# Two layers of sliding-window attention and gated MLP on one core: nine ring units, the edge visit third, and smaller edge and V buffers

## The chip, the cores and the metric

The kernel runs on one core of a Trainium2 chip. The metric is the device time of one execution in microseconds, as the median over several executions.

## The reference

A tensor x of 2048 positions by 512 features passes twice through the same two blocks, with the same weights both times: `x = x + A(layernorm(x))`, then `x = x + B(layernorm(x))`.

- A is attention with 32 heads of 16 features over a causal window of 256 positions: `qkv = x @ wqkv`; scores `q k^T / 4`, masked to `0 <= query - key < 256`; softmax; times v; then `@ wo`.
- B is a gated MLP of width 1792: `h = sigmoid(x @ w_gate) * (x @ w_up)`, then `h @ w_down`.

Everything is stored in bf16.

## The kernel before

**Tiles.** Positions are cut into 16 tiles of 128 for each layer; j counts the 32 tiles of both layers. Q, K and the normalized rows are made for groups of four tiles (512 positions). For a tile of 128 keys, only the queries of this tile and the next two can see it. These are six half tiles of 64 queries: four of them lie inside the band and are stored in the score ring, and the two at its ends (the first half of the key tile itself and the last half of the tile two later) each matter for half of the keys. Those two ends are done together, as the edge.

**Visits.** The scores of a key tile are made in five visits, in an order that `visit_list` writes out. An A visit (number `cq`, 0 to 3) takes a quarter of the heads and four half tiles of queries: it fills all four score banks (`Sps`) with products on 32-row strips of TensorE (L1066). An R visit makes the edge for all heads (L1077). After each visit, ACT takes the exponential of all 2048 columns in one instruction (L1119) and writes it to `PTring` or to `edge`. The last tile of a layer has an R and an S visit (L1087). VectorE then multiplies by the masks (L997).

**Ring units.** `PTring` holds, for each head, `UNITS` slots of 64 queries. `UNIT[j]` names the four slots of tile j, in the order of the half tiles. A visit writes its slots in ascending order. Where the ascending order is not the order of the queries, or where the ring of queries `qT` wraps, `scores` cuts the visit into contiguous runs (`cut`); each run costs 8 products and 8 weight loads. `unit_table` searches for a table that keeps the slots free of collisions.

**Values.** When all exponentials and masks of a tile's window are there, `values` multiplies by V with a column of ones (L1146), for half of the heads at a time. `pv_done[tile, half]` tells of its end. From it, ring slots (`ring_free`), edge slots (`edge_slot`) and V buffers (`VP` pairs of tiles) become free. The result is turned by a DMA (or by TensorE for the first two tiles), divided by the sum, turned again and multiplied by wo (L929).

**MLP.** Gate and up products are L834, tanh is on ACT (L852), the multiplication on VectorE (L860), the down product L898. The groups of tiles for it are listed in `GLU`, and `OPT["g0"]` and `OPT["g2"]` choose one list for each layer.

**Order.** A planner (`Plan`) runs when the program is built. It keeps a model of the five engines and of the DMA queues; whenever a modelled engine is free, it issues the ready task of the best priority (`PRIO`, later `LATE_PRIO`). `pick` decides what TensorE does next: a visit when its pace (`PACE`) and the exponential before it allow, values when they are ready, otherwise a product of an open unit of Q, K (L736, L769), V (L806), wo, gate, up or down, by rank. Where nothing is ready at the start it issues products on the identity (L1329). So each engine has a fixed instruction stream, and in the program every instruction waits for its own semaphores.

**Start.** `loads` issues the first four tiles of x (`OPT["x0"]` chooses in which pieces), then the weights of K and of Q, each half on SP and half on ACT (L491). The layer norm of a tile is statistics on VectorE (L625, L626), an epsilon and a power on POOL (L634, L635), the application on VectorE (L653), and then a turn by TensorE (L674) or by DMA (L692). `by_tile` units of Q and K go through the group's four tiles one by one and can begin before all four are there; `OPT["bq"]` and `OPT["bk"]` say how many.

Of the kernel before, what the change touches and what calls it, by code (L numbers as in the profile page):

```python
# [13 lines left out]
P = 128  # L14
# [12 lines left out]
UNITS = 8  # L27
# [3 lines left out]
VP = 6  # L31
# [4 lines left out]
def unit_table():  # L36

    def taken(table, j):
        busy = set()
        late = j > 0 and (j - 1) % NT >= NT - 2
        for i in range(max(0, j - 3), j):
            for k, u in enumerate(table[i]):
                if i + (k + 1) // 2 >= j - late:
                    busy.add(u)
        return busy

    def choices(free, t):
        for x in sorted(free):
            if t == NT - 1:
                yield (x,)
            for a in range(1, UNITS):
                if t == NT - 2 and {x + a, x + 2 * a} <= free:
                    yield (x, x + a, x + 2 * a)
                for b in range(a + 1, UNITS):
                    quad = (x, x + a, x + b, x + a + b)
                    if t < NT - 2 and set(quad) <= free and (a == 1 or b == 2 * a or 2 * b == UNITS):  # L60
                        for q in permutations(quad):
                            if q[1] < q[2]:
                                yield q

    def extend(table):
        if len(table) == 2 * NT:
            return table
        for c in choices(set(range(UNITS)) - taken(table, len(table)), len(table) % NT):
            full = extend(table + [c])
            if full:  # L70
                return full
        return None

    return extend([])


UNIT = unit_table()


# [14 lines left out]
def pool_ns(n):  # L94
# [5 lines left out]
GLU = [[[1] * 4 + [4], [1] * 4 + [2] * 2, [1] * 6 + [2], [1] * 8], [[4] * 3 + [2, 1, 1], [4] * 3 + [2, 2], [4] * 4]]  # L100
PACE = [2621, 3006, 2055, 2786, 22]
# [9 lines left out]
RATE = ((10000, 280.0), (1e9, 345.0))  # L111
FIRST = 1500
# [6 lines left out]
PRIO = dict(st_x0=9.66, ap_x0=5.2, xt_x0=4.11, st_x1=6.83, ap_x1=4.97, xt_x1=-3.99, st_x=7.22, ap_x=1.33,  # L119
    xt_x=-1.25, st_p=4.93, ap_p=3.21, xt_p=5.11, st_g=6.44, ap_g=2.28, xt_g=4.67, st_g0=1.93, ap_g0=2.34,  # L120
    xt_g0=2.83, tp=5.29, tp_g=-2.14, q=6.35, q0=1.85, q1=2.88, k=3.53, k0=0.63, k1=0.73, s=-1.61, s0=0.46,
    s1=5.56, v=-1.31, v0=3.84, v1=8.0, vv=4.71, exp=4.44, exp0=6.15, m0=4.27, m00=-2.03, e0=3.94, e00=6.05,
    e1=4.23, e10=4.3, m2=0.81, m20=21.82, th=2.08, mu=-0.98, dn=2.02, add=5.32, add0=5.49, out=5.31, mv=6.36,
    mv0=3.86, oq=6.63, oq0=3.3, no=0.56, no0=0.37, on=-0.26, on0=4.14, vc=4.31, vc0=-2.12)
OPT = dict(gu='SP', g1=1, bk=1, bq=1, wide=0, r0=2, g0=1, g2=2, x0=2, eps=0, hold=0, own=0)
SLACK = dict(xt=1080, oq=240, on=28, vc=2480)
RANK = dict(tp=-2.963, o=1.872, lead=10.494, far=6.876, v=1.959, g=2.363, d=3.317, feed=14.564, x3=44361,
    wd=12, go=211)
LATE_PRIO = dict(st_p=4.07, ap_p=2.35, xt_p=6.18, st_x=1.67, ap_x=5.19, xt_x=-0.8, st_g=2.98, ap_g=1.19,
    xt_g=5.62, q=3.84, k=3, s=3, v=0.28, exp=3, m0=4.62, e0=1.63, e1=6, m2=6.84, th=3.38, mu=3.54, dn=2.85,  # L130
    add=0.69, out=5.87, mv=5.22, oq=0.1, no=4, on=1.28, vc=3.04)
LATE_SLACK = dict(xt=0, oq=1051, on=203, vc=0)
LATE_RANK = dict(tp=-2, o=1.5, lead=10, far=5.293, v=1.796, g=1.974, d=2.466, feed=22.042, go=1418)
# [271 lines left out]
class Net:  # L405


    def __init__(self, ctx, tc, A_x, wqkv, wo, w_gate, w_up, w_down, out):
# [28 lines left out]
        self.edge = big.tile([P, 6, H // 2, HP], BF16, name="edge")  # L437
# [290 lines left out]
    def q_unit(self, L, g, cq):  # L728
        nc, pl, key = self.nc, self.pl, ("p", L, g)
        t0, gi = g * NBG, L * NTG + g  # L730

        by_tile = L == g == 0 and cq < OPT["bq"]
        w = P if by_tile else TGW

        def steps(bank):
            return [(mm_ns(w), lambda kt=kt, o=o: nc.tensor.matmul(  # L736
                self.banks[bank][:, o:o + w], lhsT=self.wq[:, kt, cq * P:cq * P + P], rhs=self.xnT[key][0][:, o // P:(o + w) // P, kt, :],
                start=kt == 0, stop=kt == KT - 1)) for o in range(0, TGW, w) for kt in range(KT)]

        def evac(u):  # L740
            u.done.then(lambda: self.used(key, 1))
            d = pl.task({"ACT": act_ns(TGW), "DVE": dve_ns(TGW)}, lambda e: self.copy(
                e, self.qT[:, cq, gi % QG * TGW:(gi % QG + 1) * TGW].rearrange("p (t z k) -> p t z k", z=2, k=HP),
                self.banks[u.bank][:].rearrange("p (t k z) -> p t z k", z=2, k=HP)), [u.done], self.prio["q" + self.phase(L, g)])
            d.done.then(self.q_ready[L, g, cq].fire)
            return d.done

        tiles = [self.xn_ready[key, t] for t in range(t0, t0 + NBG)]
        needs = [self.has_wq["q"]] + ([] if by_tile else tiles)
        if gi >= QG:  # L750
            needs.append(self.seen[divmod((gi - QG) * NBG + NBG - 1, NT)])
        u = Unit(("q", L, g, cq), steps, needs, False, evac)
        if by_tile:
            u.want = [e for e in tiles for kt in range(KT)]
        return u

    def k_slots(self, j, n):
        a = min(n, KS - j % KS)
        return [(0, a, j % KS)] + ([(a, n - a, 0)] if n > a else [])

    def k_unit(self, L, g, cq):
        nc, pl, key = self.nc, self.pl, ("p", L, g)
        t0, gi = g * NBG, L * NTG + g

        by_tile = L == g == 0 and cq < OPT["bk"]
        w = P if by_tile else TGW

        def steps(bank):
            return [(mm_ns(w), lambda kt=kt, o=o: nc.tensor.matmul(  # L769
                self.banks[bank][:, o:o + w], lhsT=self.wq[:, kt, D + cq * P:D + cq * P + P], rhs=self.xnT[key][0][:, o // P:(o + w) // P, kt, :],  # L770
                start=kt == 0, stop=kt == KT - 1)) for o in range(0, TGW, w) for kt in range(KT)]

        def evac(u):
            u.done.then(lambda: self.used(key, 1))
            slots = self.k_slots(gi * NBG, NBG)

            def cp(e):
                for a, n, at in slots:
                    self.copy(e, self.kTp[:, cq, at:at + n, 0, :], self.banks[u.bank][:].rearrange("p (t k) -> p t k", k=P)[:, a:a + n, :])

            def split(e):
                for a, n, at in slots:
                    kt = self.kTp[:, cq, at:at + n]
                    for i in (1, 0):
                        nc.vector.tensor_scalar(out=kt[:, :, i, :], in0=kt[:, :, 0, :], scalar1=self.rms[i][:, 0:1], scalar2=None, op0=ALU.mult)  # L785

            a = pl.task({"ACT": act_ns(TGW), "DVE": dve_ns(TGW)}, cp, [u.done], self.prio["k" + self.phase(L, g)])
            b = pl.task({"DVE": 300 + 320 * len(slots)}, split, [a.done], self.prio["s" + self.phase(L, g)], port=True)
            b.done.then(self.k_ready[L, g, cq].fire)
            return a.done  # L790

        tiles = [self.xn_ready[key, t] for t in range(t0, t0 + NBG)]
# [3 lines left out]
        u = Unit(("k", L, g, cq), steps, needs, False, evac)  # L796
# [147 lines left out]
    def visit_list(self):  # L944
# [4 lines left out]
        for L in range(2):  # L949
            for t in range(NT):  # L950
                if t == NT - 1:
                    self.visits += [(L, t, "R", 0), (L, t, "S", 0)]
                    continue
                for cq in range(NCQ):
                    if cq == (OPT["r0"] if t == 0 else 0):
                        self.visits.append((L, t, "R", 0))
                    self.visits.append((L, t, "A", cq))

    def visit_needs(self, L, t, kind, i):
        needs = []  # L960
        for cq in ((i,) if kind == "A" else range(NCQ)):
            needs.append(self.k_ready[L, t // NBG, cq])
            for g in {t // NBG, min(NT - 1, t + 2) // NBG}:
                needs.append(self.q_ready[L, g, cq])
# [7 lines left out]
    def visit_exp(self, s):  # L972
# [9 lines left out]
        elif j >= 2:  # L982
            deps += [self.pv_done[divmod(j - 2, NT) + (h,)] for h in range(2)]
# [35 lines left out]
    def edge_slot(self, j, z):  # L1019
        return 2 + j % 4 if z else j % 2  # L1020
# [182 lines left out]
    def by_pe(self, L, t):  # L1203

        return L * NT + t < 2 or L * NT + t >= 2 * NT - 0
# [244 lines left out]
    def go(self, *srcs):  # L1450
# [12 lines left out]
        self.q_ready = {k + (c,): Event() for k in LG for c in range(NCQ)}  # L1463
        self.k_ready = {k + (c,): Event() for k in LG for c in range(NCQ)}
# [5 lines left out]
        for L, g in LG:  # L1470
            self.left["p", L, g] = 2 * NCQ + NBG
# [18 lines left out]
        for L, g in LG:  # L1490
            for cq in range(NCQ):
                ks.append(self.k_unit(L, g, cq))
                qs.append(self.q_unit(L, g, cq))
# [66 lines left out]
```

## Time and profile before

| | us |
|---|---|
| median of 6 runs | 543.67 |
| lowest and highest | 542.39, 545.09 |
| the profiled execution | 542.42 |
| its span, first to last instruction | 540.7 |
| TensorE busy in it | 532.3 |
| VectorE busy | 410.6 |
| ScalarE (ACT) busy | 384.2 |

The span is what the profile shows; the profiled execution's own time lies 1.7 us above it. PE stands for products on TensorE, PEld for its weight loads, DVE for VectorE, ACT for ScalarE, POOL for GpSimd, SP for SyncE, which issues most DMAs. A q behind an engine's name is its sequencer. "L1066" is a line of the kernel before. In a group's row the figures are: instructions, busy time in us, mean length of one in ns, and the idle time of the engine ahead of them. In the timeline the first two figures are the start and the length of a run of like instructions, whose first shape is the one printed. In the waits the three figures are the total in us, the number of times, and the longest.

### The profile page before, as it was taken

The page shows a single profiled execution, that of the slowest core. Times are in us where ns is not written, and L with a number is a line of the kernel's source. Part 1 is how long each engine was busy: PE and PEld are TensorE (multiplying, and loading weights), DVE is VectorE, ACT ScalarE, POOL GpSimd, SP SyncE. Part 2 cuts the span into 40 slices and gives each one's busy share as a digit, 9 for nine tenths or more (in the row PEclk, how much of TensorE's full clock was granted, in tenths as well). Part 3 has the DMA queues.
Part 4 walks back from the last instruction along what each step waited for, and adds up shares of the span by engine and source line. Part 5 has one row for each costly group of instructions (what it writes and reads, how often), then busy time and mean ns, then how long its engine had stood idle before and what let it go on. Part 6 is the DMA issues. An engine that isn't in the chain of part 4 may idle for free.

```text
span 540.7 us, 22638 instructions
## 1 busy us (share of the span) xinstructions
PE 532.3 (98%) x10298; PEld 288.3 (53%) x10298; DVE 410.6 (76%) x816; ACT 384.2 (71%) x374; POOL 45.0 (8%) x105
## 2 busy tenths in 40 slices
PE   7999999999999999999999999999999999999997
PEld 7446765867667554444444455544444444444443
DVE  6999989888888797698978788797777785552332
ACT  3998879889889787797679885788868774321320
POOL 6210201000001010001000001010000000000000
PEclk9999999999999999999999999999999999999999
DMA  8862232243311433172224420242223313211001
GB/s 271 306 139 100 42 71 42 65 81 54 71 44 33 82 41 62 26 118 51 42 32 71 80 53 20 38 98 51 52 52 80 42 41 70 51 19 35 6 11 39
DMA packets 95040, 36.31 MB, mean 67 GB/s; under 512 B 78304, under 2 KB 93920, under 8 KB 94944
## 3 DMA queue, kind: packets, MB, share of 16 engines
q1 hardware_dynamic: 93584, 33.56, 29.5%
q8 instruction: 80, 1.31, 1.0%
q10 hardware_dynamic: 1360, 1.31, 0.7%
q14 instruction: 16, 0.13, 0.1%
HBM read 9.70 MB, written 2.10 MB: 22 GB/s over the span
## 4 chain that ended last, share of the span: by engine, by line
PE 92%; DMA 3%; DVE 2%; ACT 2%; issue 1%; SPq 0%; POOL 0%; DVEq 0%; ACTq 0%
PE bank L834 36%; PE bank L898 18%; PE bank L1146 9%; PE Sps L1066 7%; PE bank L929 5%; PE bank L769 5%; PE bank L736 5%; PE bank L806 4%; PE Sps L1077 2%; DMA wq<-in_A_wqkv_dram 1%; ACT PTring L1119 1%; DMA xnT<-xn 1%; DMA OnT<-On 1%; SPq L491 0%; DVE kTp L785 0%
## 5 line engine op out<-in xcount | busy, mean ns | idle before, releaser
L1119 ACT ACTIVATE PTring<-Sps 128x2048 bf16<-128x2048 f32 (+1 forms) x122 | 226.2, 1854 | 61.7 <-PE Sps L1066 57.1
L834 PE MATMUL bank<-xnT,wg 128*128 128x512 bf16 (+2 forms) x672 | 126.0, 309 | 0.2 <-DMA xnT<-xn 0.2
L834 PE MATMUL bank<-xnT,wu 128*128 128x512 bf16 (+2 forms) x672 | 124.3, 308 | 0.0
L860 DVE SCALAR_TENSOR_TENSOR hT<-hT,bank 128x512 bf16<-128x512 bf16 (+1 forms) x140 | 78.8, 576 | 42.4 <-PE bank L834 36.0
L898 PE MATMUL bank<-wd,hT 128*128 128x512 bf16 (+2 forms) x462 | 109.8, 373 | 0.0
L852 ACT ACTIVATE hT<-bank 128x512 bf16<-128x512 f32 (+1 forms) x140 | 68.8, 517 | 52.2 <-PE bank L834 50.7
L834 PEld LDWEIGHTS <-wg 128*128 128x128 bf16 x672 | 55.3, 98 | 40.9 <-issue 1.5
L834 PEld LDWEIGHTS <-wu 128*128 128x128 bf16 x672 | 55.9, 98 | 39.4 <-issue 1.0
L898 PEld LDWEIGHTS <-hT 128*128 128x128 bf16 x462 | 42.7, 98 | 46.7 <-issue 0.4
L1119 ACT ACTIVATE edge<-Sps 128x2048 bf16<-128x2048 f32 (+1 forms) x32 | 56.7, 1773 | 12.9 <-PE Sps L1077 12.6
L997 DVE TENSOR_TENSOR PTring<-PTring,mask 128x1024 bf16<-128x1024 bf16 x64 | 43.9, 687 | 25.0 <-ACT PTring L1119 24.8
L1146 PE MATMUL bank<-PTring,Vaug 128*32 128x64 bf16 (+1 forms) x2880 | 52.8, 203 | 0.4 <-issue 0.4
L1066 PEld LDWEIGHTS <-kTp 32*128 32x128 bf16 x1984 | 25.6, 93 | 45.3 <-issue 43.3
L1146 PEld LDWEIGHTS <-Vaug 128*32 128x32 bf16 x2880 | 44.3, 97 | 9.6 <-issue 5.9
L1066 PE MATMUL Sps<-qT,kTp 32*128 32x64 bf16 (+3 forms) x1984 | 48.1, 215 | 0.9 <-issue 0.6
L634 POOL TENSOR_SCALAR st<-st 128x2 f32<-128x2 f32 (+1 forms) x37 | 13.1, 353 | 427.6 <-DVE st L626 427.6
L625 DVE BATCH_NORM_STATS2 st<-xsb 128x6 f32<-128x512 bf16 x64 | 43.9, 686 | 2.6 <-DMA xsb<-in_A_x_dram 2.2
L1146 PE MATMUL bank<-edge,Vl 128*32 128x64 bf16 x1024 | 44.4, 193 | 0.1
L704 DVE CAST OTs<-bank 128x512 bf16<-128x512 f32 x48 | 34.9, 728 | 8.6 <-PE bank L1146 8.6
L1146 PE MATMUL bank<-edge,Vh 128*32 128x64 bf16 x896 | 40.8, 193 | 0.3 <-issue 0.3
L997 DVE TENSOR_TENSOR edge<-edge,maske 128x1024 bf16<-128x1024 bf16 x60 | 40.4, 680 | 0.8 <-ACT edge L1119 0.7
L997 DVE TENSOR_TENSOR PTring<-PTring,maskn 128x1024 bf16<-128x1024 bf16 x56 | 38.1, 683 | 0.0
(71 smaller groups left out, 528.6 us busy)
## 6 DMA issues: line engine op xcount, KB each, us to landing
Vl<-Vaug SPq DMA_DIRECT2D x32, 68.0 KB, 2.4
out_dram<-xsb SPq DMA_DIRECT2D x15, 128.0 KB, 2.1
Vh<-Vaug SPq DMA_DIRECT2D x28, 68.0 KB, 2.5
wg<-in_B_w_gate_dram SPq DMA_DIRECT2D x2, 896.0 KB, 9.1
wu<-in_B_w_up_dram SPq DMA_DIRECT2D x2, 896.0 KB, 11.8
wd<-in_B_w_down_dram SPq DMA_DIRECT2D x7, 256.0 KB, 4.9
xsb<-in_A_x_dram SPq DMA_DIRECT2D x6, 256.0 KB, 7.3
wq<-in_A_wqkv_dram ACTq DMA_DIRECT2D x2, 256.0 KB, 5.7
```

The lines of the kernel that those rows point to most:

```text
L625: nc.vector.bn_stats(out=st[:, 0:6], in_=self.xsb[:, t, :])
L704: self.nc.vector.tensor_copy(out=out, in_=in_)
L736: return [(mm_ns(w), lambda kt=kt, o=o: nc.tensor.matmul(self.banks[bank][:, o:o + w], lhsT=self.wq[:, kt, cq * P:cq * P + P], rhs=self.xn ...
L769: return [(mm_ns(w), lambda kt=kt, o=o: nc.tensor.matmul(self.banks[bank][:, o:o + w], lhsT=self.wq[:, kt, D + cq * P:D + cq * P + P], rhs ...
L834: return [(mm_ns(w), lambda i=i, j=j, fc=fc, wt=wt, kt=kt: self.nc.tensor.matmul(pt[:, i, j, :], lhsT=wt[:, kt, fc * P:(fc + 1) * P], rhs= ...
L852: self.nc.scalar.activation(out=self.hT[:, ch[0] * GW:ch[0] * GW + size], in_=pt, func=AF.Tanh, scale=0.5)
L860: self.nc.vector.scalar_tensor_tensor(out=h, in0=h, scalar=1.0, in1=pt, op0=ALU.add, op1=ALU.mult)
L898: nc.tensor.matmul(self.banks[bank][:, 0:w], lhsT=self.hT[:, at:at + P], rhs=self.wd[:, fc, d], start=fc == 0, stop=fc == FC - 1)
L997: done = pl.task({"DVE": dve_bf_ns(1024)}, lambda e: nc.vector.tensor_tensor(out=r, in0=r, in1=m.to_broadcast([P, 16, HP]), op=ALU.mult), ...
L1066: nc.tensor.matmul(self.sps[:, m, o:o + n * HP], lhsT=kTp[32 * m:32 * m + 32, i, tt, e, :], rhs=self.qT[32 * m:32 * m + 32, i, q0:q0 + n * ...
L1119: nc.scalar.activation(out=out, in_=src, func=AF.Exp, scale=scale)
L1146: nc.tensor.matmul(o, lhsT=Va[:, c0:c0 + 32], rhs=p(h), start=k == 0 or t == 0, stop=k == len(parts) - 1 or t == 0, tile_position=(0, 32 * g))
```

## The change

- `UNITS` goes from 8 to 9, and the searched table is replaced by a table written out. With nine slots nearly all tiles get their four in the order of the queries.
- The R visit stands third in every tile (before the A visit with `cq` 2); before, it stood so in the first tile of each layer alone and was first in the others.
- The edge buffer has 5 slots instead of 6 (two for one end, three for the other instead of four). The exponential of an R visit waits for the values of the tile before (before: of the tile two before).
- V has five pair buffers instead of six.
- Q and K are told ready tile by tile and no longer by group: a visit needs K of its own tile and Q of its own and the next two tiles. The first two Q units of the first group can be cut into three tiles and one.
- Options at the start: three pieces of x instead of two (`x0=1`), three K units and two Q units of the first group by tile (`bk=3, bq=2`; before, one and one), the epsilon of the first group added on VectorE (`eps=1`), the first transposes in banks of their own (`own=1`).
- The last MLP group of layer two is two groups of two tiles (`g2=1`; before, one of four).
- The planner's paces, priorities, ranks and its model of the DMA rate at the start have other values. `turn=2` is what was there before.

```diff
-UNITS = 8
+UNITS = 9
-VP = 6
+VP = 5
...
-UNIT = unit_table()
+UNIT = [
+    (4, 5, 7, 8), (1, 2, 3, 4), (0, 1, 5, 6), (2, 3, 7, 8), (0, 1, 4, 5), (7, 2, 3, 6), (0, 1, 7, 8), (2, 3, 4, 5),
+    (1, 2, 6, 7), (1, 3, 4, 0), (1, 2, 5, 6), (3, 4, 7, 8), (0, 1, 2, 3), (4, 5, 6, 7), (0, 1, 2), (8,),
+    (3, 4, 5, 6), (0, 1, 7, 8), (2, 3, 4, 5), (1, 2, 6, 7), (1, 3, 4, 0), (1, 2, 5, 6), (3, 4, 7, 8), (1, 2, 3, 0),
+    (4, 5, 6, 7), (1, 2, 3, 4), (0, 1, 5, 6), (2, 3, 7, 8), (0, 1, 4, 5), (2, 3, 6, 7), (0, 1, 2), (8,),
+]
...
-PACE = [2621, 3006, 2055, 2786, 22]
+PACE = [2682, 3207, 1600, 2511, 23.52]
...
-RATE = ((10000, 280.0), (1e9, 345.0))
-FIRST = 1500
+RATE = ((3300, 330.0), (5300, 160.0), (1e9, 345.0))
+FIRST = 1100
...
-OPT = dict(gu='SP', g1=1, bk=1, bq=1, wide=0, r0=2, g0=1, g2=2, x0=2, eps=0, hold=0, own=0)
+OPT = dict(gu='SP', g1=1, bk=3, bq=2, wide=0, r0=2, g0=1, g2=1, x0=1, eps=1, hold=0, own=1, ck=0, cq=2,
+    turn=2)
...
-        self.edge = big.tile([P, 6, H // 2, HP], BF16, name="edge")
+        self.edge = big.tile([P, 5, H // 2, HP], BF16, name="edge")
...
+    def cut(self, L, g, cq, n):
+        return ((0, NBG - 1), (NBG - 1, 1)) if L == g == 0 and cq < n else ((0, NBG),)
...
-            d.done.then(self.q_ready[L, g, cq].fire)
+            d.done.then(lambda: [self.q_ready[L, t, cq].fire() for t in range(t0, t0 + n)])
...
-                    if cq == (OPT["r0"] if t == 0 else 0):
+                    if cq == OPT["r0"]:
                         self.visits.append((L, t, "R", 0))
...
-            needs.append(self.k_ready[L, t // NBG, cq])
-            for g in {t // NBG, min(NT - 1, t + 2) // NBG}:
-                needs.append(self.q_ready[L, g, cq])
+            needs.append(self.k_ready[L, t, cq])
+            needs += [self.q_ready[L, u, cq] for u in range(t, min(NT, t + 3))]
...
-        elif j >= 2:
-            deps += [self.pv_done[divmod(j - 2, NT) + (h,)] for h in range(2)]
+        elif j >= 1:
+            deps += [self.pv_done[divmod(j - 1, NT) + (h,)] for h in range(2)]
...
-        return 2 + j % 4 if z else j % 2
+        return 2 + j % 3 if z else j % 2
```

## The prediction

> **What bounds the kernel now.** I read the engine shares first, then the chain that ended last, then the products by shape, then TensorE's timeline, and last the first 13 us. From the page, parts 1, 2 and 4:
>
> ```profile
> PE 532.3 (98%) x10298; PEld 288.3 (53%) x10298; DVE 410.6 (76%) x816; ACT 384.2 (71%) x374; POOL 45.0 (8%) x105
> PEclk9999999999999999999999999999999999999999
> PE 92%; DMA 3%; DVE 2%; ACT 2%; issue 1%; SPq 0%; POOL 0%; DVEq 0%; ACTq 0%
> ```
>
> TensorE is busy from start to end, unthrottled, and is 92% of the chain. Busy time hides small stops in overlapping instructions, so I took the distances from one product's start to the next from the timeline. They are rigid: 216 ns between products 512 wide, 109 at 256, 56 at 128. TensorE is one belt: the span is the sum of what lies on it, the start before it runs, and 3.4 us after the last product (537.3 to 540.7). The stops on it are few. The waits of TensorE, all that were listed above 0.2 us:
>
> ```profile
> PE bank L1329 <- POOL ident L544: 1.4, 1, 1.4
> PE bank L1146 <- issue: 0.6, 2, 0.4
> PE Sps L1066 <- issue: 0.6, 1, 0.6
> PE bank L769 <- DMA wq<-in_A_wqkv_dram: 0.5, 1, 0.5
> PE bank L736 <- DMA wq<-in_A_wqkv_dram: 0.4, 1, 0.4
> ```
>
> Summing every distance that exceeds its normal one gives 3.0 us after 12.35 us. That, the start, and the products' own cost are all that an edit can move.
>
> **What the Trainium skill says.** "TensorE: Matmul & The Clock Gate", section "Wait — 56ns, not 53.3ns?", gives N/2.4 + 2.5 ns from start to start when warm, twice the array time when cold. The trace agrees: 216, 109 and 56; the filler products on the identity stand 107 apart until about 5.3 us. The same page, Part 3, section "The mechanism", has four 32-row tiles start about 4 ns apart and run together; here I read 3 to 4 ns within a group of four. "TensorEngine Tiling (Array Packing)", section "Key Properties", says that a change of tiling mode drains TensorE. The trace agrees: from a 512-wide product to the first score product are 312 ns instead of 216, so 96 ns. These three make a score visit cheap to cut and dear to enter.
>
> **The cuts of the visits.** Of a visit's queries each contiguous run costs 8 products and 8 weight loads. From the tables of ring units in both versions, with the wrap of the query ring of 24, I counted runs: before, 28 visits of tile 0 to 14 have one run of four (8 products), 52 have two (16), 20 have three (24), 12 have four (32), and 8 have one run of three. That is 1984 products, as the page's L1066 count has. After: 84, 24, 4, 0 and 8, which is 1216. So 768 products and 768 loads go. What is one worth? By form:
>
> ```profile
> L1066 PE MATMUL Sps<-qT,kTp 32*128 32x64 bf16 x1120 | 29.1, 190 | 0.6 <-issue 0.6
> L1066 PE MATMUL Sps<-qT,kTp 32*128 32x192 bf16 x480 | 21.8, 243 | 0.0
> L1066 PE MATMUL Sps<-qT,kTp 32*128 32x256 bf16 x224 | 11.1, 273 | 0.0
> ```
>
> The mean lengths tempt: 32 at 190 against 8 at 273. They overlap, so they are no price. The timeline has it, in start times (us) of a visit and of what follows it:
>
> ```profile
> 129.21 0.40 PE L1066 MATMUL Sps<-qT,kTp 32*128 32x256 bf16 x8
> 129.54 0.61 PE L834 MATMUL bank<-xnT,wu 128*128 128x256 bf16 x4
> ...
> 155.63 0.41 PE L1066 MATMUL Sps<-qT,kTp 32*128 32x64 bf16 x32
> 155.98 0.39 PE L834 MATMUL bank<-xnT,wu 128*128 128x256 bf16 x2
> ...
> 179.32 0.37 PE L1066 MATMUL Sps<-qT,kTp 32*128 32x64 bf16 x25
> 180.27 0.23 PE L1066 MATMUL Sps<-qT,kTp 32*128 32x64 bf16 x7 [0.58 <-issue]
> ```
>
> Eight products hold the belt 0.33 us, thirty-two 0.35. Medians over all visits: 329, 334, 340 and 344 ns for one to four runs, 275 for the run of three. Visits before: 28 x 329 + 52 x 334 + 20 x 340 + 12 x 344 = 37.5 us; after: 84 x 329 + 24 x 334 + 4 x 340 = 37.0 us. **-0.5 us**. The exponential of a visit (1.88 us for ring and edge alike) and its writes are unchanged. The third pair shows what else dense products can cost: two visits of four runs met a stop of 0.58 us that waits for nothing but issue. With 64 instructions fewer in a row there, I take it as gone: **-0.6 us**, bounds 0 and -1.5 (all four issue stops of that kind, the two larger in the rows above and 0.3 to 0.6 in between).
>
> **The other products.** Two K units and one Q unit of the first group go by tile: 16 x 56 = 896 ns instead of 4 x 216 = 864, three times: **+0.1 us**. The cut of Q's first group falls on units that go by tile anyway: nothing on the belt, two more copies on ACT or DVE (0.59 or 0.69 at full width), beside the products. The last MLP group of the second layer becomes two of two tiles: 224 products of 256 for 112 of 512, 224 x 109.5 against 112 x 216.5: **+0.3 us**. It can start sooner, but from 461 us on TensorE has no gap to fill, so the sooner start is worth nothing. The end stays 3.4 us: the last down product's split is not touched.
>
> **The start.** This is the largest term. The chain in order of time:
>
> ```profile
> 2.47 0.65 SPq L491
> 3.12 0.05 issue
> 3.17 7.51 DMA wq<-in_A_wqkv_dram
> 10.68 0.04 issue
> 10.72 0.51 PE bank L736 x6
> 11.23 0.22 PE bank L1329 x4
> 11.45 0.24 PE bank L674 x4
> 11.69 0.02 issue
> 11.71 0.59 ACT xnT L702
> 12.31 0.04 issue
> 12.35 0.38 PE bank L769 x4
> ```
>
> K's weights are there at 9.21 us, Q's at 10.72. Only one K and one Q unit could run by tile, tile 3's transposes stood in TensorE's queue behind Q products waiting for the weights (its normalized rows were ready at 9.84, its transposes began at 11.29), and the belt runs without filler only from 12.35. By then it had done 16 transposes, 12 K and 12 Q products, 40 x 56 = 2.2 us. After: three K units by tile have 48 products, 2.7 us, between the K and the Q weights. The added pair of x loads (one issue more on SP and one on ACT, 0.8 us each) is ahead of both weights on both queues; as the DMA engines are the limit from 5 us on (331 to 382 GB/s), I charge half, 0.4 us: K's weights at 9.6, Q's at 11.1. The epsilon on VectorE takes POOL's step out (0.32 us from its start to the next step's), and tile 0's normalization no longer stands behind tile 2's statistics (root done 5.82, applied 6.83); transposes are out of the way before 9.6. From 9.6 to 12.35 the belt then does 2.75 us on top of 0.9 us of transposes: 3.65 - 2.24 = **-1.4 us**. Bounds: -1.8 with no later weights; +0.8 if the pair delays them in full and the order of the queue wastes the rest.
>
> **Entries.** A block of value products that follows a visit pays no 96 ns of its own; 55 of 63 do so now. The new order can win or lose the other 8: -0.8 to +0.8 us, taken as nothing.
>
> **The moved edge visit.** Its 32 products (346 ns), exponential and two masks (0.68 us each on DVE) are the same, in third place. Its exponential now waits for both halves of the values of the tile before, where it waited for the tile two before; behind it on ACT stand copies and tanh, and the next visit's products, which need the score banks. In the trace of before the third visit's exponential starts 2.5 us (median) after the second half of the values of the tile before has ended; in two of 28 tiles (3 and 5) it starts 0.7 us sooner than that. So it binds twice: cost between 0 and 1.4 us, and MLP products are there to fill: nothing. V in five pairs: a V unit now waits for values seven tiles back instead of nine; in the trace only tiles 10, 12 and 13 of layer 0 were written before that point, by 9 to 13 us. Their 12 products (2.6 us) move later, into MLP work: nothing, at most the 0.2 us of a late transpose each. The steps of the planner (paces 2.68 and 3.21 us, priorities) order other work. Attention may end some 10 us later than at 457; from 461 on there are 76 us of pure MLP, so that is covered.
>
> **Sum.** -0.5 - 0.6 - 1.4 + 0.1 + 0.3 = -2.1 us, on the profiled execution's 542.42: 540.3. Its time lies 1.25 under the median of the runs, so the median goes from 543.67 to 541.5.
>
> **Rivals.** *The start gives nothing.* The added x loads push the weights back by their full 0.8 us, which eats what the K units by tile bring. For it: the chain's one long piece is the weights' DMA. Against: half of that piece is bandwidth shared with loads behind it. Then -0.5 + 0.4 and little of the issue stop: 543.0 to 543.7, within what can be told. *The edge visit's new wait (slower).* Place: ACT at the third visit of each tile, once per tile on 30 tiles. The trace's evidence is one visit for whose score banks TensorE had to wait for ACT, 0.25 us, at 26.69 us. If each edge visit met that, 30 x 0.25 = 7.5 us, less 2.1: 549. It decides from 3.8/30 = 0.13 us per tile on; at half the price, 545.3. For it: the slack of 2.5 us is under one visit and the early pace is planned tighter, 1.6 us. Against: filler work is ready. *It doesn't do what it says:* the tables were counted, and wide visits come out; but "wide" is worth 5 ns a run.
>
> **How the numbers follow.** No change is within 0.3%, 1.63 us, about what a measurement of this kernel can tell. Forecast 0.58, its own range 538.0 to 542.2: below, the other 2.4 us of stops gone, the start at its better bound (0.4) and the entries saved (0.8), 537.9; above, half of the start's gain missing (0.7). Nothing 0.18. Slower 0.24, mostly 545 to 549. The range of 8 in 10 reaches to the middle of the last: 538.0 to 546.0.
>
> **What would show it.** Right: about 9680 products (10298 - 768 + 36 + 112), L1066 at 1216, a wide visit still 0.33 us; products without filler from about 10 us; stops after that under 3 us. Wrong: Q or K weights landing after 11.5; waits of TensorE for ACT at L1066 or L1077 above 2 us in sum; a gap of TensorE after 461 us.

## The result, and the profile after

| | before | after |
|---|---|---|
| median, us | 543.01 (37 runs) | 541.66 (18 runs) |
| lowest and highest | 541.6, 545.09 | 540.87, 542.47 |
| span of the profiled execution | 540.7 | 539.7 |
| products on TensorE | 10298 | 9658 |

The ratio is 0.9972, with an interval of 0.9964 to 0.9981: faster by 0.28%. The forecast was 541.5 us, 0.40% less than before. The gain is certain and small; whether it is over the 0.3% named in the prediction can't be told. The median came out close partly by luck: the forecast stood on six runs of the kernel before, with a median of 543.67, and the 37 runs here give 543.01, from which the same -2.1 us would have led to 540.9. So each term of the sum is looked at below.

Engine shares, granted clock and chain shares of the page after, which answer to the three lines shown first in the prediction:

```profile
PE 531.4 (98%) x9658; PEld 293.1 (54%) x9658; DVE 420.4 (78%) x844; ACT 382.2 (71%) x380; POOL 43.3 (8%) x99
PEclk9999999999999999999999999999999999999999
...
PE 89%; DVE 5%; ACT 2%; DMA 1%; issue 1%; POOL 0%; SPq 0%; ACTq 0%; POOLq 0%
```

TensorE is still the belt, the engine whose work in a row makes up the span. The count of products is the forecast 9678 less 20 filler products. In the chain, DVE has 5% where it had 2%: a first sign that stops may have moved. The waits of TensorE say which (line, what it waited for; us in all, times, longest):

```profile
PE bank L1292 <- POOL ident L508: 1.4, 1, 1.4
PE Sps L1029 <- ACT PTring L1082: 1.1, 4, 0.4
PE Sps L1040 <- issue: 0.6, 1, 0.6
PE bank L638 <- DVE xn L617: 0.5, 2, 0.3
PE bank L638 <- ACT qT L666: 0.4, 1, 0.4
PE bank L734 <- DMA wq<-in_A_wqkv_dram: 0.3, 1, 0.3
```

In the kernel after, L1029 is the product of an A visit (before, L1066), L1040 that of an R visit, L638 the transpose of normalized rows. The waits for weights and issue have shrunk from 2.1 us to 0.9, and waits for ACT and DVE have come in. They lie early: the transposes of tiles 4 to 7, and score products at 44.7, 91.6, 134.6 and 137.2 us. The timeline (start, length of a run of like instructions; in brackets the idle time before it and its cause) has the first three:

```profile
18.68 0.88 PE L638 MATMUL bank<-ident,xn 128*128 128x128 bf16 x8 [0.40 <-ACT qT L666]
...
21.45 0.40 PE L638 MATMUL bank<-ident,xn 128*128 128x128 bf16 x4 [0.23 <-DVE xn L617]
...
25.37 0.40 PE L638 MATMUL bank<-ident,xn 128*128 128x128 bf16 x4 [0.28 <-DVE xn L617]
```

At the start the chain now runs through work of TensorE where it stood on the weights:

```profile
3.02 5.42 DMA wq<-in_A_wqkv_dram
8.44 0.05 issue
8.49 0.73 PE bank L734 x10
9.22 0.22 PE bank L1292 x4
9.44 0.06 PE bank L734
9.50 0.24 PE Sps L638 x4
```

The SP half of K's weights is there at 8.44 us (before, 9.17), products of K by tile follow at once, and only four filler products (L1292) stand between them. Last, the A visits by form. The row with 256 columns went from 224 products to 672, the row with 64 from 1120 to 256:

```profile
L1029 PE MATMUL Sps<-qT,kTp 32*128 32x256 bf16 x672 | 33.4, 273 | 0.3 <-ACT PTring L1082 0.2
L1029 PE MATMUL Sps<-qT,kTp 32*128 32x192 bf16 x256 | 11.7, 245 | 0.5 <-ACT PTring L1082 0.5
L1029 PE MATMUL Sps<-qT,kTp 32*128 32x64 bf16 x256 | 9.2, 189 | 0.4 <-ACT PTring L1082 0.4
```

**The account of the belt.** I summed the distances from one product's start to the next in both traces, as in the prediction, and split them into a normal distance and a stop:

| term, us | forecast | measured |
|---|---|---|
| score products, own time | -0.5 | -0.5 |
| full-array products (by tile, last group) | +0.4 | +0.36 |
| stops of issue after 12.35 us | -0.6 | -0.6 (1.22 to 0.62) |
| start (useful work by 12.35 us: 2.24, then 3.98) | -1.4 | -1.74 |
| entries into narrow modes (160 in both) | 0 | 0 |
| other stops after 12.35 us | 0 | +1.65 |
| after the last product | 0 | -0.18 |
| sum | -2.1 | -1.0 |

So four terms hold within 0.1 us and the end within 0.2, the start gave 0.3 us more, and 1.65 us of new stops took nearly all of the start's gain back. The idle time of TensorE before its products after 12.35 us shows where: ended by ACT, it went from 0.36 to 1.81 us; by DVE, from 0.24 to 0.74; by DMA, from 0.27 to nothing; by nothing but issue, from 1.22 to 0.62.

### The profile page after: what moved, and what is told of

It reads as the page before. It is cut to its first block, busy times and chain, and to the rows that moved or that the text cites. A ratio compares the mean times of both kernels' runs of the same rounds, so it can differ in the third digit from the quotient of the medians.

```text
span 539.7 us, 21359 instructions
## 1 busy us (share of the span) xinstructions
PE 531.4 (98%) x9658; PEld 293.1 (54%) x9658; DVE 420.4 (78%) x844; ACT 382.2 (71%) x380; POOL 43.3 (8%) x99
## 4 chain that ended last, share of the span: by engine, by line
PE 89%; DVE 5%; ACT 2%; DMA 1%; issue 1%; POOL 0%; SPq 0%; ACTq 0%; POOLq 0%
PE bank L798 37%; PE bank L862 18%; PE bank L1109 9%; PE Sps L1029 7%; PE bank L893 5%; PE bank L734 4%; PE bank L770 3%; PE bank L703 3%; PE Sps L1040 2%; ACT PTring L1082 1%; DMA wq<-in_A_wqkv_dram 1%; DVE kTp L749 1%; DVE st L589 1%; DVE PTring L960 1%; DVE edge L960 1%
## 5 line engine op out<-in xcount | busy, mean ns | idle before, releaser
L798 PE MATMUL bank<-xnT,wu 128*128 128x512 bf16 (+2 forms) x728 | 128.2, 297 | 0.0
L798 PE MATMUL bank<-xnT,wg 128*128 128x512 bf16 (+2 forms) x728 | 128.2, 298 | 0.0
L824 DVE SCALAR_TENSOR_TENSOR hT<-hT,bank 128x256 bf16<-128x256 bf16 (+1 forms) x154 | 80.8, 537 | 33.9 <-ACT hT L816 21.2
L816 ACT ACTIVATE hT<-bank 128x256 bf16<-128x256 f32 (+1 forms) x154 | 71.2, 482 | 48.5 <-PE bank L798 48.3
L798 PEld LDWEIGHTS <-wg 128*128 128x128 bf16 x728 | 60.7, 98 | 36.8 <-issue 2.5
L798 PEld LDWEIGHTS <-wu 128*128 128x128 bf16 x728 | 61.4, 98 | 34.5 <-issue 2.5
L668 DVE CAST OTs<-bank 128x512 bf16<-128x512 f32 x59 | 43.0, 729 | 21.7 <-PE bank L1109 21.4
L1029 PE MATMUL Sps<-qT,kTp 32*128 32x256 bf16 (+3 forms) x1216 | 47.4, 248 | 1.2 <-ACT PTring L1082 1.1
L598 POOL TENSOR_SCALAR st<-st 128x2 f32<-128x2 f32 (+1 forms) x33 | 10.7, 324 | 443.7 <-DVE st L590 443.7
L1029 PEld LDWEIGHTS <-kTp 32*128 32x128 bf16 x1216 | 18.2, 92 | 45.4 <-issue 43.5
```

Source lines behind the costliest of these rows:

```text
L668: self.nc.vector.tensor_copy(out=out, in_=in_)
L798: return [(mm_ns(w), lambda i=i, j=j, fc=fc, wt=wt, kt=kt: self.nc.tensor.matmul(pt[:, i, j, :], lhsT=wt[:, kt, fc * P:(fc + 1) * P], rhs= ...
L816: self.nc.scalar.activation(out=self.hT[:, ch[0] * GW:ch[0] * GW + size], in_=pt, func=AF.Tanh, scale=0.5)
L824: self.nc.vector.scalar_tensor_tensor(out=h, in0=h, scalar=1.0, in1=pt, op0=ALU.add, op1=ALU.mult)
L1029: nc.tensor.matmul(self.sps[:, m, o:o + n * HP], lhsT=kTp[32 * m:32 * m + 32, i, tt, e, :], rhs=self.qT[32 * m:32 * m + 32, i, q0:q0 + n * ...
```

## Experiments

Each time below stands beside runs of the kernel before on the same chip. "Useful" is the work of TensorE, filler left out, by 12.35 us; "stops" are those after it. Before has 2.24 and 6.2, after 3.98 and 7.3; these sums take in more than the 3.0 us of the prediction, and only their differences are used. Each kernel has one trace, and in five traces with the start and the order of after (after, e_cut4, e_cut2, e_stat, e_g2) useful work lies between 3.42 and 4.70 us, so differences of some tenths there are no finding. (Some traces lack about 80 product records; each gap looks like 0.2 us of issue, and these are left aside.)

**e_cut4: the wide visits cut up again, in the same order.**

```diff
+            kept = len(cut)
+            cut = [(at + x, pos + x, 1) for at, pos, n in cut for x in range(n)]
...
-            return pl.count(8 * len(runs)) or 220
+            return pl.count(8 * kept) or 220
```

> The changed kernel with every A visit cut into runs of one half tile: 32 products (24 in tiles 14 and 30) instead of 8 to 24, and the planner told the old counts, so that the order on all engines stays as it is. Theory (a run costs 5 ns): 84 visits x 15 ns + 24 x 10 + 4 x 4 + 8 x 12 = 1.6 us on TensorE, and issue stops as before the change or a little more, 1 to 3 us: 543 to 546 us. Rival (price by the products' mean length, or by the instruction count): 2624 more products at 15 ns or more each, above 580 us. Rival (cuts cost nothing, hidden): 541.7.

Measured: 549.78 us, ratio 1.0128 (1.0106 to 1.0150), span 547.4, useful 4.70, stops 13.65. The score products' own time rose by 2.03 us where 1.6 was forecast; the median visit went from 329 ns to 344, so the price of some 5 ns a run stands. The stops rose by 6.4 us, where the theory had allowed 1 to 3 us of stops of issue. The waits of TensorE:

```profile
PE Sps L1031 <- issue: 1.5, 4, 0.5
PE bank L798 <- issue: 1.5, 4, 1.0
...
PE bank L1110 <- issue: 1.0, 3, 0.7
```

"issue" is time in which the engine waited for nothing that the profile shows. The theory fell short, and both rivals missed; a new theory was needed: TensorE's instructions themselves come late. Stops of issue over 0.27 us make 4.4 us here and 0.6 in after, so they account for 3.8 of the 6.4 us; the rest is not accounted for.

**e_cut2: the same with two runs of two, 736 products more and not 2560.**

```diff
+            if kept == 1:
+                at, pos, n = cut[0]
+                cut = [(at, pos, 2), (at + 2, pos + 2, n - 2)]
```

> The changed kernel with every A visit that is one run cut into two, the planner told the old counts, so the order on all engines stays. It puts the score products back to 1952, close to the 1984 of the kernel before, and nothing else: the worth of the wide visits in their own order. Theory (5 ns a run on TensorE, and the rest by instruction fetch, in proportion to e_cut4's 6.1 us of added stops for 2560 products): 84 x 5 ns = 0.5 us of products and about 1.5 us of stops, most of them put down to issue: 542.8 to 544.5. Rival (only the products' time counts; e_cut4's stops come from its densest stretches alone): 542.0 to 542.4, stops of TensorE within 0.5 us of the changed kernel's 8.2.

Measured: 544.38 us, ratio 1.0041 (1.0028 to 1.0053), span 543.5, useful 3.53, stops 10.2. By the two ratios this is 0.69% or 3.7 us more than after, of which the products' own time is 0.45. Two stops carry most of the rest:

```profile
84.74 1.04 PE L893 MATMUL bank<-wot,OnT 128*128 128x512 bf16 x4 [1.43 <-DMA OnT<-On]
...
106.91 0.55 PE L798 MATMUL bank<-xnT,wg 128*128 128x128 bf16 x7 [1.15 <-issue]
```

The first waits for a DMA transpose issued at 80.19 that took 4.51 us. An instruction transfer started at 82.1, while the transpose was under way; in after none starts between 79.1 and 84.3. The second has an instruction transfer that ended 1.4 us before it. The theory of instruction fetch held for the second stop; for the first, one transfer at the same time is all that speaks for it. (Some 0.45 us are later weights at the start; the edit does not touch these loads.)

**Is it instruction fetch?** The page counts the instruction transfers of TensorE's queue, one for 256 instructions:

```profile
q8 instruction: 75, 1.23, 0.9%
```

That is after; before has 80, e_cut2 81, e_cut4 95. I then took every stop of "issue" over 0.27 us after 12.35 us in all fourteen traces (before, after, and the kernels of this section): there are 23. Each ends 1.2 to 1.6 us after the end of an instruction transfer (one, 2.0). That window of 0.4 us, 80 times, covers 6% of a span; 22 of 23 stops end in it. Their sum is 0.96 us in before, 0.62 in after, 4.38 in e_cut4, and nothing in e_x2, f_after and f_best. This is a coincidence in time that chance can hardly make; the runs that add products raise it, and no run moved the transfers alone.

**e_ring and e_start: one part of the change alone, on the kernel before.** e_ring takes the nine slots and their table, the edge third with five slots, and the five V pairs; e_start the options at the start and the planner's DMA rates; Q and K are still told ready by group in both.

```diff
-UNITS = 8
+UNITS = 9
...
-                    if cq == (OPT["r0"] if t == 0 else 0):
+                    if cq == OPT["r0"]:
```

```diff
-OPT = dict(gu='SP', g1=1, bk=1, bq=1, wide=0, r0=2, g0=1, g2=2, x0=2, eps=0, hold=0, own=0)
+OPT = dict(gu='SP', g1=1, bk=3, bq=2, wide=0, r0=2, g0=1, g2=2, x0=1, eps=1, hold=0, own=1)
```

> The kernel before with the ring alone: nine units, the table written out, the edge visit third in every tile, five edge slots, five V pairs; options at the start, tail, paces and priorities as before. Theory (the ring is worth 0.5 us of products plus fewer issue stops, and an order that is not fitted to it loses more): score visits 0.5 us cheaper on TensorE, but stops of TensorE larger by 2 us or more: 543 to 550 us. Rival (the ring alone carries the gain): 541 to 542. Rival (the edge visit's new wait is dear): stops of TensorE for ACT at the score products of 3 us or more.

> The kernel before with the start alone: three pieces of x, three K and two Q units by tile, epsilon on VectorE, own banks, the planner's DMA rates of the changed kernel; ring, tail, paces and priorities as before. Theory (the start itself saves 2 us up to 12 us, whatever follows): filler plus stops before 12.35 us smaller by 1.5 to 2 us, K's weights landed near 8.4 us; the total depends on the order after it, 541 to 547 us. Rival (the start's gain comes from the new priorities): filler and stops before 12.35 us as before.

Measured: e_ring 549.5 us, ratio 1.0130 (1.0107 to 1.0152), stops 15.5; e_start 552.76 us, ratio 1.0180 (1.0159 to 1.0201), useful 3.25, stops 20.0. Both parts alone make the kernel slower. For e_ring that is inside its forecast; e_start had 541 to 547 us, with 1.5 to 2 us won at the start, and won 1.0. In e_ring the waits of TensorE are for ACT:

```profile
PE Sps L1029 <- ACT edge L1082: 2.7, 2, 2.1
PE Sps L1029 <- ACT PTring L1082: 2.5, 5, 1.0
...
PE Sps L1040 <- ACT PTring L1082: 1.2, 1, 1.2
```

This is the sign that the rival of the edge visit had named, but not its mechanism: the exponential of the third visit starts 1.8 us or more after the values that it waits for. The timeline has the place:

```profile
93.35 0.41 PE L1040 MATMUL Sps<-qT,kTp 32*128 32x64 bf16 x32 [1.23 <-ACT PTring L1082]
95.83 0.41 PE L1029 MATMUL Sps<-qT,kTp 32*128 32x64 bf16 x16 [2.06 <-ACT edge L1082]
```

Two visits follow each other with no product of other work between them: no filler was ready. The order that the planner writes with priorities made for another kernel leaves TensorE idle there.

The stops are not all of it. The clock that TensorE was granted, in tenths for 40 slices of the span (9 is 90% or more), is full from 7.0 us to the last product in before and after. In e_ring (first line) and in f_start (second line; the kernel follows below) it is not:

```profile
PEclk9999999799999999999999999999999999999999
PEclk9999899999999999999999999999999999999999
```

In e_ring the granted clock is half from 97.3 to 104.1 us, from 1.4 us after the stop of 2.06 us shown above, and products of 128 columns stand 107 ns apart in place of 56. In e_start it is half from 101.4 to 104.8, after a stop of 2.03 us. So about 3.4 us of e_ring's 9.3 us of added stops, and 1.7 of e_start's 13.8, are products at half clock. Every run of the two shows it (mean clock 0.991 to 0.997, and 0.999 or 1.0 in every run of before).

**f_before, f_ring, f_start, f_after: each of the four with its order fitted anew.** The planner's priorities, ranks, slacks and paces were searched again for each, on the planner's own model, as in this cut of f_after:

```diff
+RANK.update(v=4.396, feed=16.768, far=4.379, lead=5.565, wd=609, go=368, g=-0.393, x3=28598, d=3.042, o=-0.447, tp=-0.566)
...
+PACE[2] = 1378.3
+PACE[4] = 23.02
+PACE[1] = 3223.94
```

> The kernel before, with nothing changed but the planner's priorities, ranks, slacks and two of its paces, fitted anew by a search in the planner's own model. Theory (the order of the streams weighs as much as any of the change's parts): it differs from before by over 0.2% in either direction, 539.5 to 545.5 us, by stops of TensorE alone; the products' own cost is the same to 0.1 us. Rival (the parts carry the gain): the same as before within 0.1%.

> The ring alone on the kernel before (nine units, table, edge visit third, five edge slots, five V pairs), with priorities, ranks, slacks and paces fitted anew to it in the same manner. Theory (e_ring lost by its unfitted order, not by the ring's waits): at least 4 of the 6.5 us that e_ring lost come back, 541 to 545.5 us, and TensorE's stops for ACT at score products fall from 6.4 us to under 2.5. Rival (the edge visit's new wait is dear in any order): they stay above 4 us, 547 or more.

> The start alone on the kernel before, priorities, ranks, slacks and paces fitted anew to it. Theory (the start is worth 1 to 2 us once the order after it fits): 540.5 to 543 us, at or under f_before. Rival (without the ring the start's gain is given back): as f_before or above it by 0.5 us or more.

> The changed kernel, priorities, ranks, slacks and paces fitted anew in the same manner, nothing else. Theory (some 8 us of stops are left on TensorE, and the order sets them): 539.5 to 542.5 us; products' own cost as in the changed kernel to 0.1 us, the difference all in stops and filler. Rival (the order is not what is left): within 0.1% of the changed kernel, 541.7.

| | median, us | ratio to before | useful | stops |
|---|---|---|---|---|
| f_before | 545.05 | 1.0038 (1.0025 to 1.0051) | 2.24 | 10.0 |
| f_ring | 546.63 | 1.0067 (1.0048 to 1.0086) | 2.41 | 11.3 |
| f_start | 547.4 | 1.0083 (1.0061 to 1.0104) | 4.26 | 13.2 |
| f_after | 539.91 | 0.9948 (0.9936 to 0.9961) | 4.31 | 6.1 |

The new order gave the ring 2.9 of its 6.5 us back and the start 5.4 of its 9.7: about half of those losses was order, and in the ring's case they are no more than its 3.4 us at half clock, which f_ring's trace does not have (two of its six runs have a mean clock of 0.996 or 0.997). Neither came out ahead of before, so the forecasts of both missed, while those of f_before and f_after held. In f_ring the waits for ACT at score products fell to 2.0 us, as forecast; a wait of 2.0 us for a DMA transpose and a stop of issue of 1.1 us stand beside them. But the same search made the kernel before itself slower by 0.38%, so differences of a few tenths of a per cent between these four are no price of a part. What they do show is which stops stay. f_start does 2.0 us more useful work by 12.35 us than before, and loses more than that to stops that wait for nothing that the profile shows:

```profile
PE bank L845 <- issue: 2.6, 1, 2.6
PE bank L1157 <- issue: 2.3, 4, 1.3
```

After the stop of 2.6 us the clock is half from 59.4 to 62.8 us, which costs 1.7 us more; all six runs of f_start have a mean clock of 0.996 or 0.997. It has narrow visits and 80 instruction transfers; f_after, with wide ones and 75, has no such stop over 0.27 us.

**e_stat: part of VectorE's early work left out.** The statistics of tiles 4 to 7 read a quarter of each row, so this kernel leaves out part of the computation.

```diff
+            part = D // 4 if key == ("p", 0, 1) else D
+            nc.vector.bn_stats(out=st[:, 0:6], in_=self.xsb[:, t, 0:part])
```

> The changed kernel with the statistics of tiles 4 to 7 of the first layer taken from a quarter of the features (part of the computation is left out), order unchanged. It takes about 4 x 0.45 = 1.8 us off VectorE between 13 and 25 us. Theory (what the start gained is given back because VectorE's normalization of tiles 4 to 7 is late for TensorE's transposes there): the stops of TensorE between 17 and 26 us, 1.5 us now, shrink to under 0.8, and the time falls by 0.4 to 1.0 us. Rival (ACT's copies or the queue's own order hold those transposes): no change, within 0.2 us.

Measured: 540.81 us, ratio 0.9958 (0.9943 to 0.9972), 0.14% under after with overlapping intervals; useful 3.42, stops 6.2. The total is as expected, though it can't be told from after; its place is not as expected. The waits for DVE at 21.4 and 25.4 us are gone, and waits for ACT stand in for them:

```profile
19.19 0.87 PE L639 MATMUL bank<-ident,xn 128*128 128x128 bf16 x8 [0.39 <-ACT qT L667]
...
23.72 0.40 PE L1030 MATMUL Sps<-qT,kTp 32*128 32x256 bf16 x8 [0.17 <-ACT edge L1083]
...
26.47 0.40 PE L1030 MATMUL Sps<-qT,kTp 32*128 32x256 bf16 x8 [0.51 <-ACT PTring L1083]
```

Between 17 and 26 us the stops went from 1.8 to 1.6 us only. So the statistics are not what this stretch is short of by themselves; with DVE relieved, ACT is late next. Which of the two would have to be relieved first stays open.

**e_g2: the last MLP group of layer two in one piece again.**

```diff
-OPT = dict(gu='SP', g1=1, bk=3, bq=2, wide=0, r0=2, g0=1, g2=1, x0=1, eps=1, hold=0, own=1, ck=0, cq=2,
+OPT = dict(gu='SP', g1=1, bk=3, bq=2, wide=0, r0=2, g0=1, g2=2, x0=1, eps=1, hold=0, own=1, ck=0, cq=2,
```

> The changed kernel with its last MLP group as one of four tiles, as before the change (112 products of 512 for 224 of 256). Theory (the split costs its products' 0.3 us and gains nothing, for TensorE has no gap there): 541.2 to 541.5, 0.2 to 0.4 us under the changed kernel. Rival (the split lets the last MLP group start while other engines would hold it up): slower than the changed kernel by 0.5 us or more, with a gap of TensorE after 460 us.

Measured: 540.95 us, ratio 0.9976 (0.9967 to 0.9985), span 540.1. It can't be told from after: 0.3 us are too little for these runs to show. The rival, 0.5 us slower or more, is out.

**e_x2: tiles 0 and 1 of x in one pair of loads, all else in the same order.**

```diff
+                if n == 1:
+                    both = slice(0, 2)
...
+                    fn = (lambda q=q, z=z, wide=wide: q.dma_start(out=self.xsb[z:P:2, 0:2, :], in_=wide)) if tiles.start == 0 else (lambda: None)
```

> The changed kernel with tiles 0 and 1 of x loaded by one pair of DMAs instead of two, in the place of tile 0's; the order of all engines' other instructions stays. So the number of x pieces alone goes back to that of the kernel before. Theory (small pieces of x land early and keep the loads that come behind K and Q back; that brings the start forward): tile 0 lands at 3.4 us or later instead of 3.2, the last of x at 5.9 or later instead of 4.9, K's last weights near 9.0 instead of 8.4, and 0.5 to 1.0 us are lost before 12.35 us: 542.0 to 542.8. Rival (one DMA less ahead of the weights brings them 0.6 us sooner, as the prediction reckoned): K's weights at 8.0 or sooner, 540.9 to 541.5. The landings scatter by 0.5 us from run to run, so the time decides only if the effect is above 0.3%.

Measured: 540.99 us, ratio 0.9949 (0.9930 to 0.9967), span 538.4, useful 4.42, stops 6.5. The start's gain doesn't need the pieces of x: without the third the SP half of K's weights landed at 7.28 us, in after at 8.44, and more useful work was done by 12.35 us, not less. The theory fell and the time is that of the rival; but useful work of 4.42 us lies within the scatter named above, so that two pieces are better is not shown. The start's gain is then from the units by tile, the epsilon and the banks, which were not tried one by one.

**f_best: f_after's search carried on, with the loads of e_x2.**

```diff
+RANK.update(feed=14.568, d=1.611, wd=372, o=-1.457, go=917, x3=29493, v=3.427, far=12.488, tp=-1.203, lead=5.55, g=1.54)
...
+PACE[2] = 1520.01
```

> The changed kernel with priorities, ranks, slacks and paces fitted longer than in f_after, and x in two pieces in the place of three as in e_x2. Theory (f_after's gain of 0.3% over the changed kernel comes from stops of TensorE and adds to what e_x2 gave): 538.5 to 540.5 us, stops under 7 us, ratio to before 0.991 to 0.995. Rival (f_after and e_x2 gained the same start, so they don't add): as f_after, ratio 0.995 or above.

Measured: 539.68 us, ratio 0.9933 (0.9919 to 0.9946), span 537.8, useful 4.31, stops 5.7. It is the fastest and beats both kernels, inside its forecast; from f_after it can't be told. Its engine shares, and its two largest waits of TensorE past the one on the identity:

```profile
PE 530.2 (99%) x9658; PEld 291.5 (54%) x9658; DVE 421.0 (78%) x845; ACT 383.0 (71%) x379; POOL 41.4 (8%) x99
```

```profile
PE Sps L1059 <- ACT PTring L1112: 0.8, 3, 0.4
PE Sps L668 <- DVE xn L647: 0.8, 1, 0.8
```

The count of products is that of after; what it gained is in the stops and the start, and no stop of issue is left.

## Why the prediction was right, and where it was wrong

**Right: the belt and its prices.** The cuts, the units by tile with the last group, and the stops of issue came out within 0.1 us of their terms. A wide visit still holds the belt for its 0.33 us:

```profile
129.20 0.40 PE L1029 MATMUL Sps<-qT,kTp 32*128 32x256 bf16 x8
129.53 0.82 PE L770 MATMUL bank<-wq,xnT 128*128 128x512 bf16 x3
```

**Right: the edge visit and V cost nothing.** The exponential of the third visit starts 1.8 us at the least, 2.7 in the median, after the second half of the values of the tile before (the last tile of a layer, whose R visit fills one end only, aside). That wait never binds, where I had two tiles bind. No V unit waits for its pair; the least slack is 4.5 us. The last exponential starts at 471.4 us (before, 456.8), and TensorE has no gap after it. The rival with 549 us is out in this order. (e_ring came to 549.5 us by another way.)

**Right in size, with one step wrong: the start, -1.74 for -1.4.** Its term charged 0.4 us for later weights. They were 0.7 to 0.9 us earlier (K's SP half 8.44, Q's last half 9.79; before 9.17 and 10.68). The reason isn't settled. The loads behind them (V's weights, and x) are issued 0.45 us later in after, which would leave them bandwidth; but e_x2 issues those at the old times and has K's at 7.28. In the five traces with the loads and their order as in after and K's landing on record (after, e_cut4, e_stat, e_g2, f_after) K's half lands between 7.67 and 8.96 us, in four with those of before (before, e_ring, f_before, f_ring) between 8.74 and 9.27. So earlier weights are likely more than chance; the 0.3 us by which the term was off may be chance altogether.

**Wrong: the other stops after 12.35 us, which the sum leaves as they were.** This is the step that failed. The start's term assumed that work done earlier is time saved to the end, and the list of what is late next stopped at 12.35 us. In its place, 1.65 us of new stops, at the transposes of tiles 4 to 7 and at early score products, where TensorE was there before ACT and DVE were ready. The prediction had the two parts in its hand, the tighter early pace (first twelve visits 2.94 us apart before, 2.85 after) and ACT's role, but put them into a rival about the edge visit instead of into the sum. That they come of being earlier is argued from their places and not shown: e_stat, which relieved DVE, moved them and hardly shrank them. The order makes a part of them. f_after, with the same products, has 6.1 us of stops where after has 7.3; 0.6 us of this is after's stop of issue, which is no matter of ACT or DVE, and waits for ACT at A visits fell from 1.1 to 0.6 us. The waits at the transposes stayed (0.9 us in both). What else would remove them stays open.

**Right in size, wrong in kind: what a wide visit is worth.** The prediction says that wide is worth 5 ns a run, and 0.5 us in all. On the belt that is so. But e_cut2 puts 736 products back, in the same order, and loses 3.7 us, eight times their own 0.45. Of this 1.15 us is a stop just after an instruction transfer, 1.43 a DMA transpose that was late beside one, and 0.45 the start's scatter. The prediction saw one stop of 0.58 us, and priced it as one event that goes. It was one of a kind that recurs in other places: the one stop of issue in after, of 0.62 us, is at an R visit at 141 us, where before has none. That the total of the term came out right is luck: it took for a place what the traces show as a matter of count and chance.

## What to carry to other kernels

Where one engine is a belt, price its products by start-to-start distances, and then ask of each microsecond won at the start which engine is late next; a start that is earlier by 1.7 us, with 0.9 us saved besides, gave 1.0 at the end of the trace here. Instructions are a resource of their own: with dense small products, count them, since 8% more cost 0.69% here, the start's scatter included, while their own time was 0.08%. Look at the granted clock before a loss is put down to waits alone: in e_ring more than a third of the added stops was half clock. An order written by a planner belongs to its kernel: of a change that comes with new priorities, its parts put alone under the old ones were slower by 1.3 to 1.8%, so test a part by undoing it with the order held, as e_cut2 does.

## What the runs showed of the hardware

**Instruction fetch.** The Trainium skill's page "Runtime: NRT & Kernel Launch", section "Instruction fetch mechanics", has instructions come in blocks of 256 over a DMA queue, with a cost that is mostly hidden. The count agrees: 75 transfers for 19316 products and weight loads. Hidden it is not always, if the stops of issue are put down to it: 23 stops of 0.27 to 2.6 us in fourteen traces, each ending 1.2 to 2.0 us after an instruction transfer, and 4.4 us of them in e_cut4.

**Transposes by DMA beside it.** I split the transposes `OnT<-On` after 100 us by whether an instruction transfer was in flight during them. Without, the median from issue to landing is 2.44 us in before, 2.43 in after and 2.44 in e_cut2; with one, 3.27, 3.21 and 3.82 (10 to 15 transposes in each group; where exactly "during" begins moves the second medians by some tenths). In a chain of values, turn and wo that has no slack this can be a stop of its own kind, as at 84.74 us in e_cut2. Which of the two delays the other was not tried.

**Half clock after long stops.** In e_ring, e_start and f_start TensorE's granted clock was half for 6.8, 3.4 and 3.4 us. These stretches began 1.4, 0.3 and 0.1 us after stops of 2.06, 2.03 and 2.62 us had ended. No stop after 12.35 us in the fourteen traces is longer than these three; after the next longest, 1.96 us in f_ring and 1.74 in e_start, the clock stayed full.
